# Seven-product gates: both partial sums as single-bank PSUM tiles, products in alternating order

## Chip, cores and metric

One core of a Trainium2 chip. The time is device microseconds (us) of one execution, and the median of several executions is compared. A profiled execution gives the trace; its span runs from its first to its last instruction.

## What is computed

A linear attention with random features (8 batches, 8 heads, 576 tokens, head size 64, 128 features) feeds a bilinear feed-forward layer over 4608 tokens:

```
phi(x) = exp(x @ omega.T - |x|^2/2 - max) / sqrt(m)
attn   = (phi(q) @ (phi(k).T @ v)) / (phi(q) @ sum(phi(k)) + 1e-6)
x      = attn as [4608, 512]
a, b   = x @ w1, x @ w2          # 512 -> 1024 each
out    = ((a * b) @ w3) @ w_out  # -> [4608, 512]
```

## The kernel before

The tokens are 36 chunks of 128. Each chunk goes through projection of q and k (tiles qpj and kpj), exponentials, the attention's quotient (tile nu), a split into fp16 high and low parts, a DMA transpose into xT, the gates (a and b, and their product) and the output projection (tile o, 24 matmuls of 128x512). The two last weights are multiplied into one matrix W at the start, while weights are converted; that head lasts until some 285 us.

Numbers are kept exact enough by splitting each operand in two fp16 parts and adding three products (PASSES). From chunk 8 on, two chunks at a time and one half i of the 1024 columns at a time (a "half pair", 28 in all), the gates use seven block products instead of eight: `seven_gate`. Each product is 24 matmuls of 128x128. Numbered in the order of the code before:

1. X = plain w1 blocks times X0; ACT copies X to s1 (snap, L1301)
2. W = plain blocks times X1; DVE adds W to s1 (plus, L1307)
3. X += sums 2 times B0; ACT copies X to u2 (L1301)
4. Y = sums 1 times A0
5. X += sums 3 times A1; ACT copies X to u3 (L1301), then DVE adds Y to u3 (L1305)
6. X += plain w2 blocks times B1; DVE multiplies s1 by X (L1340), and s1 is split into h
7. Y += sums 4 times C0; DVE adds Y to u2 (L1307), multiplies u2 by u3 (L1344, DVE or POOL), and u2 is split into h

Products 1, 2 and 6 read the weights from w12b; 3, 4, 5 and 7 read sums that lie in the arena. X and Y are the two banks of one PSUM tile xy with tag "pa" (shape 128 x 2 x 512 f32); W is a one-bank tile w with tag "pm". There are two pa buffers (four banks) and four pm buffers (four banks). Attention (qpj, kpj, nu, the k-v sums) takes pa buffers; output projections, norms, the first chunks' gates and filler matmuls ("warm", which keep PE running in the head where nothing is ready) take pm buffers.

The order of all instructions is written out ahead by a list scheduler (class Plan): each operation has costs per engine, what it reads and writes, the buffers it takes and a rank. At each instant an idle engine takes the ready operation of lowest rank whose buffers are free. Ranks are a base per chunk plus a shift per step from the table SHIFT. The scheduler keeps X and Y apart, as keys (xy, 0) and (xy, 1). Each engine then executes its list strictly in that order and waits on semaphores, which the tile framework sets from the tiles that an instruction reads and writes. Reads of gate results have the gate's rank less 1000, ahead of all else that is ready on their engine.

The small buffers u (two of them, for u2 and u3) and asb (two, for s1) are the other ones that gates hold.

Of the kernel before, what the change touches and what calls it, by code (L numbers as in the profile page):

```python
# [53 lines left out]
class Plan:  # L54
# [215 lines left out]
    "attend": [-140.6108, -1279.0332, 96.048, -814.6063, 46.0223, 565.0647, 888.1831, -189.2611, -1755.0403, -492.3028, -593.491, -657.8477, -700.7601, -33.1091, -308.4841, -242.0773, -417.6381, -346.2611, 1.1496, -638.2965, -706.1053, -102.5187, 7.911, 97.4165, -119.6369, -950.2856, -491.3768, 237.9438, 549.924, -177.7823, 68.1437, -180.35, 127.2563, 10.4704, -299.7041, -19.7196],  # L270
    "fetch": [-422.5336, -193.7664, -115.3316, -55.3051, -40.5138, -42.8211, -11.7789, -8.9557, 0.0, -10.1416, 3.4931, 0.0, -5.8054, -27.3038, -12.3339, -12.1842, 7.0423, 8.1052, 12.6868, -5.6312, 0.0, 1.5375, 21.7423],
    "gate": [84.4841, -9.8224, 184.0693, 825.4235, 328.6051, -313.6299, 281.3475, 611.0941, -290.9896, -117.7816, -64.9002, -270.3623, 1.1389, -19.5741, 3.9425, 16.0617, -2.4194, 4.5289, 0.0, 0.0, -13.2021, -13.3977, 0.0, 0.0, -30.4327, -0.4898, 0.0, 0.0, -27.3399, 22.7329, 0.0, 0.0, 3.0654, 10.6963, 0.0, 0.0, -96.6277, 1.1412, 0.0, 0.0, 6.7892, 20.0692, 0.0, 0.0, -108.4898, 7.294, 0.0, 0.0, 8.1194, 460.834, 0.0, 0.0, -155.6188, -94.2281, 0.0, 0.0, -181.6658, 83.4966, 0.0, 0.0, 99.2112, 1108.5741, 0.0, 0.0, 371.8924, 602.2299, 0.0, 0.0, -618.141, 814.4092],
# [9 lines left out]
    "out": [908.8765, 99.9845, 133.0496, -21.1332, -0.2109, 18.3999, 0.0586, 4.1794, -128.2247, -4.2684, -1.2544, -1.3084, -129.2248, 28.5423, 3.7214, 23.152, -1.7608, 11.9693, 12.9972, 547.9276, 861.8305, 278.0591, 393.7249, 61.9603, 499.264, 809.9431, 201.8663, -36.053, 36.4142, -127.9741, 1115.7242, 51.6774, 1069.562, 459.4601, 67.1902, 204.5781],  # L282
# [5 lines left out]
    "sum": [311.8865, -32.354, 244.6241, 473.4846],  # L288
    "unit": [-821.4058, -181.9305, -184.3904, -88.8633, -132.9001, -47.9472, -28.52, -5.7077, -171.7387, 20.0538, 28.6707, -182.3521, -50.1462, -60.8755, -11.3478, -7.7281, 80.6276, 111.3257, 279.8563, 284.0477, -32.0859, 306.7812, 422.9414, -290.3398, -63.7105],
    "v": [0.0, 0.0, 852.8931, -29.537, 21.5041, -411.0284, 56.0495, -1895.7559],  # L290
# [42 lines left out]
def tile_favor_attention_then_bilinear_ffn(  # L333
# [128 lines left out]
    def one(e, us, fn, **kw):  # L462
        return op([(e, us, fn)], **kw)
# [743 lines left out]
    sums = {}  # L1207
# [52 lines left out]
    def seven_gate(c0, i, rank):  # L1260

        xy, w = Buf("pa", f"xy_{c0}_{i}"), Buf("pm", f"w_{c0}_{i}")

        def plain(n, c):
            return lambda: w12[n][i][c], ("b", i, n * NC + c)
# [11 lines left out]
        def product(dst, key, ws, x, start, new=()):  # L1277
            xv, xkey = x

            def go():  # L1280
                for f in range(4):
                    mm = [(c, a, b) for c in range(2) for a, b in PASSES]
                    for j, (c, a, b) in enumerate(mm):
                        nc.tensor.matmul(  # L1284
                            dst()[:, f * P : (f + 1) * P], ws[c][0]()[:, a, f * P : (f + 1) * P], xv(c, b),
                            start=start and f == 0 and j == 0, stop=j == len(mm) - 1, skip_group_check=True,
                        )

            one(PE, 1.35, go, r=[x_[1] for x_ in ws] + [xkey] + (everything if xy in new else []), w=[key], new=new, rank=rank)

        X, Y, Wd = (lambda: xy.ap[:, 0]), (lambda: xy.ap[:, 1]), (lambda: w.ap)
        kx, ky, kw = (xy, 0), (xy, 1), (w, 0)
# [4 lines left out]
        def f32(b):  # L1297
            return b.ap

        def snap(t, scale):  # L1300
            one(ACT, 0.58, lambda: nc.scalar.mul(f32(t), X(), scale), r=[kx], w=[t], new=[t], rank=first)  # L1301
# [27 lines left out]
        product(X, kx, [plain(0, 0), plain(0, 1)], block("X", 0), True, [xy])  # L1329
# [349 lines left out]
```

## Time and profile before

| | us |
|---|---|
| median of 3 runs | 808.61 (807.83 to 812.87) |
| profiled execution, its time | 807.72 |
| its span | 805.7 |
| PE busy | 765.6 (95%) |
| DVE busy | 640.9 (80%) |
| ACT busy | 487.9 (61%) |
| POOL busy | 293.5 (36%) |

PE is TensorE's matmuls, DVE is VectorE, ACT is ScalarE, POOL is GpSimd. The rest of the profiled execution's time, 2.0 us, lies around the span. The mean granted TensorE clock is 0.994 of full speed.

### The profile page before, as it was taken

The numbers are of one execution on the slowest core, as the hardware profiler recorded it, in microseconds if no ns is written. First come the engines' busy times: TensorE is split into PE (matmuls) and PEld (weight loads), VectorE is DVE, ScalarE is ACT, GpSimd is POOL, SyncE is SP. The second block draws the span as 40 slices with busy tenths as digits, with TensorE's granted clock in tenths as the row PEclk, the third lists the DMA queues.
The fourth block names the chain that finished last, engine by engine and source line by source line (L and its number), as shares of the span: only waits on it lengthen the run. The fifth ranks groups of instructions, "written<-read, shape, count | busy, mean of one in ns | idle before, by whom it ended". The sixth has DMA issues, their size and how long they took to land.

```text
span 805.7 us, 24557 instructions
## 1 busy us (share of the span) xinstructions
PE 765.6 (95%) x10475; PEld 595.6 (74%) x10475; DVE 640.9 (80%) x1169; ACT 487.9 (61%) x948; POOL 293.5 (36%) x327
## 2 busy tenths in 40 slices
PE   9999999989999998999998999998999999999998
PEld 7845478866887677777967877785878877768874
DVE  6899998999968897898798897987688767576321
ACT  5675876687789878565865666654566534442222
POOL 2010146356435343354153433474344323132210
PEclk9899999999999999999999999999999999999999
DMA  9978863524545675356543555463425543433201
GB/s 332 293 224 273 231 170 42 120 55 112 126 88 145 132 153 106 68 100 126 134 93 86 108 114 112 93 113 78 89 55 117 89 76 72 67 92 61 47 15 53
DMA packets 166909, 93.82 MB, mean 116 GB/s; under 512 B 136976, under 2 KB 145296, under 8 KB 166800
## 3 DMA queue, kind: packets, MB, share of 16 engines
q1 hardware_dynamic: 158784, 79.60, 44.1%
q10 hardware_dynamic: 8016, 12.65, 4.9%
q8 instruction: 82, 1.34, 0.7%
q14 instruction: 27, 0.22, 0.1%
HBM read 49.50 MB, written 9.44 MB: 73 GB/s over the span
## 4 chain that ended last, share of the span: by engine, by line
PE 53%; DVE 22%; ACT 11%; DMA 7%; issue 5%; POOL 2%; POOLq 0%; SPq 0%; ACTq 0%; DVEq 0%
PE xy L1284 20%; PE o L1511 12%; PE wp L1131 4%; PE ab L1177 3%; PE w L1284 2%; PE kvp L804 2%; ACT junk L486 2%; DMA qraw<-qT 2%; DMA vraw<-v 2%; PE qpj L618 1%; PE nu L889 1%; PE kvp L751 1%; PE kpj L611 1%; DVE vhl L734 1%; ACT e_q L648 1%
## 5 line engine op out<-in xcount | busy, mean ns | idle before, releaser
L1284 PE MATMUL xy<-xT,arena 128*128 128x128 f16 x2688 | 166.2, 219 | 11.3 <-ACT asb_s L1301 9.8
L1284 PEld LDWEIGHTS <-arena 128*128 128x128 f16 x2688 | 154.0, 98 | 16.8 <-issue 13.6
L1284 PEld LDWEIGHTS <-w12b 128*128 128x128 f16 x2016 | 115.5, 98 | 18.4 <-issue 9.2
L1177 PE MATMUL ab<-xT,w12b 128*128 128x128 f16 (+1 forms) x1152 | 89.8, 240 | 3.1 <-ACT asb L1189 2.8
L1284 PE MATMUL xy<-xT,w12b 128*128 128x128 f16 x1344 | 84.3, 219 | 8.8 <-DVE u_u L1305 4.6
L1177 PEld LDWEIGHTS <-w12b 128*128 128x128 f16 x1152 | 82.2, 99 | 10.3 <-issue 4.2
L1511 PE MATMUL o<-Wb,w12b 128*128 128x512 f16 x384 | 88.3, 379 | 0.5 <-ACT o L1520 0.4
L1511 PEld LDWEIGHTS <-w12b 128*128 128x128 f16 x384 | 36.0, 98 | 40.8 <-issue 0.8
L1511 PE MATMUL o<-Wb 128*128 128x512 f16 x252 | 58.1, 379 | 0.0
L1511 PE MATMUL o<-Wb,arena 128*128 128x512 f16 x228 | 52.5, 379 | 2.1 <-DVE asb L1191 1.8
L1301 ACT ACTIVATE u_u<-xy 128x512 f32<-128x512 f32 x56 | 33.1, 590 | 35.4 <-PE xy L1284 33.9
L1340 DVE TENSOR_TENSOR asb_s<-xy,asb_s 128x512 f32<-128x512 f32 x28 | 19.3, 690 | 41.2 <-PE xy L1284 37.5
L669 POOL TENSOR_TENSOR ek<-e_k,ek 128x1024 f16<-128x1024 f32 x18 | 40.4, 2243 | 28.5 <-ACT ek L526 20.1
L631 DVE TENSOR_REDUCE nm_q<-qpj 128x8 f32<-128x1024 f32 x36 | 43.7, 1215 | 2.7 <-PE qpj L618 2.0
L631 DVE TENSOR_REDUCE nm_k<-kpj 128x8 f32<-128x1024 f32 x36 | 43.7, 1214 | 2.7 <-PE kpj L611 1.8
L669 POOL TENSOR_TENSOR eq<-e_q,eq 128x1024 f16<-128x1024 f32 x15 | 32.9, 2194 | 34.3 <-ACT eq L526 15.8
L1511 PEld LDWEIGHTS <-Wb 128*128 128x128 f16 x252 | 23.6, 98 | 27.2 <-issue 1.1
L1284 PE MATMUL w<-xT,w12b 128*128 128x128 f16 x672 | 42.1, 219 | 1.4 <-DVE asb_s L1307 1.4
L659 ACT ACTIVATE e_q<-e_q,ln_e,es_q 128x1024 f32<-128x1024 f32 x25 | 30.9, 1238 | 17.2 <-DVE e_q L655 13.9
L1520 ACT ACTIVATE o<-o,oscs 128x512 f32<-128x512 f32 x36 | 24.6, 682 | 27.3 <-PE o L1511 23.8
L1511 PEld LDWEIGHTS <-arena 128*128 128x128 f16 x228 | 21.3, 98 | 26.4 <-issue 2.7
L1305 DVE TENSOR_TENSOR u_u<-xy,u_u 128x512 f32<-128x512 f32 x28 | 19.2, 686 | 24.4 <-ACT u_u L1301 24.3
(235 smaller groups left out, 1644.2 us busy)
## 6 DMA issues: line engine op xcount, KB each, us to landing
vraw<-v SPq DMA_DIRECT2D x36, 260.0 KB, 3.5
qraw<-qT SPq DMA_DIRECT2D x36, 256.0 KB, 2.9
kraw<-kT SPq DMA_DIRECT2D x36, 256.0 KB, 3.2
out<-o SPq DMA_DIRECT2D x36, 256.0 KB, 2.2
arena<-w3T ACTq DMA_DIRECT2D x6, 1024.0 KB, 5.6
arena<-w ACTq DMA_DIRECT2D x6, 1024.0 KB, 5.4
arena<-wo SPq DMA_DIRECT2D x4, 1024.0 KB, 8.1
arena<-w3T SPq DMA_DIRECT2D x2, 1024.0 KB, 7.5
```

Source lines behind the costliest of these rows:

```text
L486: nc.scalar.activation(d, src, AF.Square, scale=pre, accum_out=dst)
L631: one(DVE, 1.22, lambda: nc.vector.tensor_reduce(nm.ap, pj(), AX.X, ALU.max, negate=True), r=[pa], w=[nm], new=[nm])
L659: one(ACT, 1.23, lambda: nc.scalar.activation(e.ap, e.ap, AF.Exp, scale=factor(), bias=ln_e), r=key, w=[e])
L669: engine(g).tensor_tensor(f16(t.ap)[:, 1], e.ap, f16(t.ap)[:, 0], ALU.subtract)
L1131: nc.tensor.matmul(bank.ap, w[:, j], guest[:, j], start=j == 0, stop=j == NF - 1)
L1177: nc.tensor.matmul(dst, w12[m][i][cc][:, a, r * P : (r + 1) * P], x.ap[:, b, cc, off : off + T], start=j == 0, stop=j == len(mm) - 1,)
L1284: nc.tensor.matmul(dst()[:, f * P : (f + 1) * P], ws[c][0]()[:, a, f * P : (f + 1) * P], xv(c, b), start=start and f == 0 and j == 0, stop ...
L1301: one(ACT, 0.58, lambda: nc.scalar.mul(f32(t), X(), scale), r=[kx], w=[t], new=[t], rank=first)
L1305: one(DVE, 0.69, lambda: nc.vector.tensor_tensor(f32(t), dst(), f32(t), ALU.add), r=[key], w=[t], rank=first)
L1340: one(DVE, 0.69, lambda: nc.vector.tensor_tensor(s1.ap, X(), s1.ap, ALU.mult), r=[kx], w=[s1], rank=first)
L1511: nc.tensor.matmul(bank.ap, hs[c, f][1]()[:, a], W[f][:, b], start=f0 + i == 0, stop=f0 + 4 == NF and i == len(mm) - 1,)
L1520: one(ACT, 0.67, lambda: nc.scalar.mul(o.ap, bank.ap, sc), r=[bank, ("osc", c)], w=[o], new=[o], rank=rank - 1000)
```

## The change

X and Y become two one-bank tiles of tag "pm", x and y, both taken by product 1. W goes away: product 2 writes Y, and product 4 starts Y again. The copy into u3 now reads Y after product 4, and the addition to u3 reads X after product 5 (before, the copy read X and the addition Y). Products 6 and 7 change places: the product with C0 into Y comes sixth and the one with B1 into X last. So the bank alternates X, Y, X, Y, X, Y, X. Numbers of matmuls, copies and additions stay, as do all buffer counts. Gates no longer take pa buffers. All entries of the table SHIFT have new values (left out but for two lines).

```diff
 SHIFT = {
-    "kv parts": [7.7168, 235.9384],
+    "kv parts": [-438.9681, -616.9088],
...
-    "sum": [311.8865, -32.354, 244.6241, 473.4846],
+    "sum": [482.7184, 151.9164, 140.7414, -351.1859],
...
     def seven_gate(c0, i, rank):
-        xy, w = Buf("pa", f"xy_{c0}_{i}"), Buf("pm", f"w_{c0}_{i}")
+        bx, by = Buf("pm", f"x_{c0}_{i}"), Buf("pm", f"y_{c0}_{i}")
...
-            one(PE, 1.35, go, r=[x_[1] for x_ in ws] + [xkey] + (everything if xy in new else []), w=[key], new=new, rank=rank)
-
-        X, Y, Wd = (lambda: xy.ap[:, 0]), (lambda: xy.ap[:, 1]), (lambda: w.ap)
-        kx, ky, kw = (xy, 0), (xy, 1), (w, 0)
+            one(PE, 1.35, go, r=[x_[1] for x_ in ws] + [xkey] + (everything if bx in new else []), w=[key], new=new, rank=rank)
+
+        X, Y = (lambda: bx.ap), (lambda: by.ap)
+        kx, ky = bx, by
...
-        def snap(t, scale):
-            one(ACT, 0.58, lambda: nc.scalar.mul(f32(t), X(), scale), r=[kx], w=[t], new=[t], rank=first)
+        def snap(t, scale, src=X, key=kx):
+            one(ACT, 0.58, lambda: nc.scalar.mul(f32(t), src(), scale), r=[key], w=[t], new=[t], rank=first)
...
-        product(X, kx, [plain(0, 0), plain(0, 1)], block("X", 0), True, [xy])
+        product(X, kx, [plain(0, 0), plain(0, 1)], block("X", 0), True, [bx, by])
         snap(s1, 2.0**-37)
-        product(Wd, kw, [plain(0, 2), plain(0, 3)], block("X", 1), True, [w])
-        plus(s1, Wd, kw, 2.0**-37)
+        product(Y, ky, [plain(0, 2), plain(0, 3)], block("X", 1), True)
+        plus(s1, Y, ky, 2.0**-37)
         product(X, kx, [(sums[2, i, c]) for c in range(2)], block("B", 0), False)
         snap(u2, 2.0**-37)
         product(Y, ky, [(sums[1, i, c]) for c in range(2)], block("A", 0), True)
+        snap(u3, 1.0, Y, ky)
         product(X, kx, [(sums[3, i, c]) for c in range(2)], block("A", 1), False)
-        snap(u3, 1.0)
-        plus(u3, Y, ky, 1.0)
+        plus(u3, X, kx, 1.0)
+        product(Y, ky, [(sums[4, i, c]) for c in range(2)], block("C", 0), False)
         product(X, kx, [plain(1, 2), plain(1, 3)], block("B", 1), False)
+        plus(u2, Y, ky, 2.0**-37)
         one(DVE, 0.69, lambda: nc.vector.tensor_tensor(s1.ap, X(), s1.ap, ALU.mult), r=[kx], w=[s1], rank=first)
         out_parts(c0, s1)
-        product(Y, ky, [(sums[4, i, c]) for c in range(2)], block("C", 0), False)
-        plus(u2, Y, ky, 2.0**-37)
```

## Rows read from the trace of the kernel before

**Rows 1.** The page, busy time, share of the span, instructions of PE.

```profile
PE   765.6 (95%) x10475; PEld 595.6 (74%) x10475; DVE 640.9 (80%) x1169; ACT 487.9 (61%) x948; POOL 293.5 (36%) x327
```

**Rows 2.** Table by stretch: length, busy time of each engine, granted clock, DMA.

```profile
0.00:285.00 285.00, 275.89 (x2909) 205.18 (x2910) 253.74 (x463) 209.91 (x477) 105.17 (x125) 0.98 0.62 167
285.00:805.70 520.70, 489.72 (x7570) 390.46 (x7566) 387.15 (x708) 277.95 (x471) 188.34 (x203) 1.00 0.43 89
...
800.00:805.70 5.70, 1.83 (x9) 0.63 (x7) 0.00 (x0) 0.70 (x2) 0.00 (x0) 0.99 0.24 92
```

**Rows 3.** Groups by line, PE: the filler matmuls (busy, mean ns, idle before).

```profile
L458 PE MATMUL warm<-ones 128*128 128x256 bf16 x127 | 18.0, 293 | 1.1 <-DVE unscaled L377 1.1
```

**Rows 4.** Who waited for whom, PE: us in total, times, longest.

```profile
PE xy L1284 <- ACT asb_s L1301: 9.8, 14, 0.7
PE xy L1284 <- DVE u_u L1305: 4.6, 6, 1.4
...
PE xy L1284 <- DVE e_q L655: 2.1, 1, 2.1
...
PE qpj L618 <- DVE xw_x L910: 1.6, 3, 0.9
PE w L1284 <- DVE asb_s L1307: 1.4, 1, 1.4
PE xy L1284 <- ACT u_u L1301: 1.1, 2, 0.7
...
PE xy L1284 <- ACT e_k L648: 0.7, 1, 0.7
PE xy L1284 <- DVE mx L923: 0.6, 1, 0.6
...
PE xy L1284 <- DVE xw_x L910: 0.5, 1, 0.5
```

**Rows 5.** Timeline near 698 us: start, length, engine, line; idle before and its releaser.

```profile
695.48 1.50 PE L1284 MATMUL xy<-xT,w12b 128*128 128x128 f16 x24
...
696.82 1.50 PE L1284 MATMUL xy<-xT,arena 128*128 128x128 f16 x24
...
698.16 1.50 PE L1284 MATMUL xy<-xT,w12b 128*128 128x128 f16 x24
698.36 0.69 DVE L1340 TENSOR_TENSOR asb_s<-xy,asb_s 128x512 f32<-128x512 f32 x1 [0.52 <-PE xy L1284]
...
699.50 1.50 PE L1284 MATMUL xy<-xT,arena 128*128 128x128 f16 x24
...
701.04 0.60 ACT L1301 ACTIVATE asb_s<-xy 128x512 f32<-128x512 f32 x1 [1.33 <-PE xy L1284]
...
701.69 1.50 PE L1284 MATMUL xy<-xT,arena 128*128 128x128 f16 x24 [0.69 <-ACT asb_s L1301]
```

**Rows 6.** Timeline near 712 us: a product behind a DVE read of the other bank.

```profile
711.37 0.60 ACT L1301 ACTIVATE u_u<-xy 128x512 f32<-128x512 f32 x1 [1.19 <-PE xy L1284]
...
712.52 0.68 DVE L1305 TENSOR_TENSOR u_u<-xy,u_u 128x512 f32<-128x512 f32 x1
...
713.26 1.50 PE L1284 MATMUL xy<-xT,w12b 128*128 128x128 f16 x24 [0.59 <-DVE mx L923]
```

**Rows 7.** Timeline near 728 us: reads of tile w and of tile xy.

```profile
726.27 1.50 PE L1284 MATMUL w<-xT,w12b 128*128 128x128 f16 x24
727.61 2.84 PE L1284 MATMUL xy<-xT,arena 128*128 128x128 f16 x48
727.88 0.69 DVE L1307 SCALAR_TENSOR_TENSOR asb_s<-w,asb_s 128x512 f32<-128x512 f32 x1 [0.47 <-PE w L1284]
...
730.49 0.60 ACT L1301 ACTIVATE u_u<-xy 128x512 f32<-128x512 f32 x1 [5.50 <-PE xy L1284]
731.14 1.50 PE L1284 MATMUL xy<-xT,arena 128*128 128x128 f16 x24 [0.69 <-ACT u_u L1301]
```

**Rows 8.** The page, groups by line: the multiplication that reads X (L1340).

```profile
L1340 DVE TENSOR_TENSOR asb_s<-xy,asb_s 128x512 f32<-128x512 f32 x28 | 19.3, 690 | 41.2 <-PE xy L1284 37.5
```

More of the change, by code (lines that the diff above doesn't have):

```diff
@@ L269 @@
 SHIFT = {
-    "attend": [-140.6108, -1279.0332, 96.048, -814.6063, 46.0223, 565.0647, 888.1831, -189.2611, -1755.0403, -492.3028, -593.491, -657.8477, -700.7601, -33.1091, -308.4841, -242.0773, -417.6381, -346.2611, 1.1496, -638.2965, -706.1053, -102.5187, 7.911, 97.4165, -119.6369, -950.2856, -491.3768, 237.9438, 549.924, -177.7823, 68.1437, -180.35, 127.2563, 10.4704, -299.7041, -19.7196],
-    "fetch": [-422.5336, -193.7664, -115.3316, -55.3051, -40.5138, -42.8211, -11.7789, -8.9557, 0.0, -10.1416, 3.4931, 0.0, -5.8054, -27.3038, -12.3339, -12.1842, 7.0423, 8.1052, 12.6868, -5.6312, 0.0, 1.5375, 21.7423],
@@ L272 @@
-    "gate": [84.4841, -9.8224, 184.0693, 825.4235, 328.6051, -313.6299, 281.3475, 611.0941, -290.9896, -117.7816, -64.9002, -270.3623, 1.1389, -19.5741, 3.9425, 16.0617, -2.4194, 4.5289, 0.0, 0.0, -13.2021, -13.3977, 0.0, 0.0, -30.4327, -0.4898, 0.0, 0.0, -27.3399, 22.7329, 0.0, 0.0, 3.0654, 10.6963, 0.0, 0.0, -96.6277, 1.1412, 0.0, 0.0, 6.7892, 20.0692, 0.0, 0.0, -108.4898, 7.294, 0.0, 0.0, 8.1194, 460.834, 0.0, 0.0, -155.6188, -94.2281, 0.0, 0.0, -181.6658, 83.4966, 0.0, 0.0, 99.2112, 1108.5741, 0.0, 0.0, 371.8924, 602.2299, 0.0, 0.0, -618.141, 814.4092],
[9 rows of a table removed]
@@ L282 @@
-    "out": [908.8765, 99.9845, 133.0496, -21.1332, -0.2109, 18.3999, 0.0586, 4.1794, -128.2247, -4.2684, -1.2544, -1.3084, -129.2248, 28.5423, 3.7214, 23.152, -1.7608, 11.9693, 12.9972, 547.9276, 861.8305, 278.0591, 393.7249, 61.9603, 499.264, 809.9431, 201.8663, -36.053, 36.4142, -127.9741, 1115.7242, 51.6774, 1069.562, 459.4601, 67.1902, 204.5781],
[5 rows of a table removed]
-    "sum": [311.8865, -32.354, 244.6241, 473.4846],
-    "unit": [-821.4058, -181.9305, -184.3904, -88.8633, -132.9001, -47.9472, -28.52, -5.7077, -171.7387, 20.0538, 28.6707, -182.3521, -50.1462, -60.8755, -11.3478, -7.7281, 80.6276, 111.3257, 279.8563, 284.0477, -32.0859, 306.7812, 422.9414, -290.3398, -63.7105],
@@ L290 @@
-    "v": [0.0, 0.0, 852.8931, -29.537, 21.5041, -411.0284, 56.0495, -1895.7559],
+    "attend": [-344.5336, -863.3505, -70.6144, -131.482, -1506.3662, -333.3574, -103.4191, 7.1947, 60.9253, -32.7535, 18.6681, -108.953, -558.1044, -52.2323, 382.9496, -190.0001, -104.0751, -91.4797, -646.8141, -687.6983, -37.7378, 211.8501, 1393.0138, 106.7495, -170.1491, -110.946, 57.5431, 184.7415, 56.0684, -192.3624, -91.951, -176.7992, 216.8146, 38.3368, -2248.693, -15.202],
+    "fetch": [-395.1367, -263.3025, -107.3478, -142.792, -36.362, -959.709, -14.3577, -14.5706, 0.0, -4.7734, 4.0789, 0.0, -17.9307, -10.2591, -11.7003, -3.8869, 17.9688, 18.5746, 3.5, 16.9483, 0.0, 12.1216, 13.06],
@@ new lines @@
+    "gate": [34.7804, -29.6444, -10.065, -89.002, -27.3084, -6.0439, 129.6502, -17.0297, 388.6957, -8.5912, 692.3104, 937.1265, 284.3371, -322.219, 193.869, 370.3877, 275.6107, 459.2977, 0.0, 0.0, 55.2125, 133.4596, 0.0, 0.0, 223.4237, 807.8211, 0.0, 0.0, -406.232, 4.2812, 0.0, 0.0, 16.9321, 150.1117, 0.0, 0.0, 56.867, 317.3446, 0.0, 0.0, 100.7986, 261.576, 0.0, 0.0, -46.2142, 104.0213, 0.0, 0.0, -222.6991, 208.6584, 0.0, 0.0, -991.9536, -55.2257, 0.0, 0.0, -325.8881, 255.4881, 0.0, 0.0, -16.8875, 305.8452, 0.0, 0.0, -15.2719, -18.917, 0.0, 0.0, -679.3126, 312.5891],
[9 rows of a table added]
@@ new lines @@
+    "out": [-20.132, -230.7836, -62.9796, 830.6893, 254.1977, 930.6871, 237.9168, -335.4428, 951.938, -341.3368, 808.7732, 348.4642, -130.897, 1115.6368, 71.106, -104.36, 322.1385, 263.4889, 289.4962, 10.9208, -596.5897, 394.1804, 557.7642, 49.388, -25.2456, 258.9955, 85.3124, -252.7556, 554.9951, 330.1611, -242.5933, 625.2243, -610.7126, -232.717, 496.3645, 207.0009],
[5 rows of a table added]
+    "sum": [482.7184, 151.9164, 140.7414, -351.1859],
+    "unit": [-747.9261, -719.9066, -200.9629, -717.993, -48.1889, -174.9094, -18.9419, -8.5076, -71.4105, -1.8121, 13.5129, -73.3507, -54.5629, -37.5469, -5.9012, 4.1535, 29.5488, 34.147, 20.2489, 96.7241, -353.4154, 184.6303, 287.0949, -149.1731, 4.9956],
@@ L291 @@
+    "v": [0.0, 0.0, 256.8978, 193.3537, 250.3211, -6.0913, -183.8097, -199.8197],
 }
```

26 rows, old and new, of the table SHIFT are left out of this document.

## The prediction, made before the change was run

> **What bounds the kernel now.** I first read the busy shares [rows 1]: PE works 765.6 us, 95% of the span of 805.7, DVE 80% and ACT 61%. So PE is the bound, and a gain must come out of its 40.1 us of idle time or out of work on it that serves nothing. The table by stretch [rows 2] splits that. Until 285 us, the head without seven-product gates, PE idles 285.0 - 275.9 = 9.1 us, and a further 18.0 us of its busy time are filler matmuls [rows 3]. From 285 us on it idles 520.7 - 489.7 = 31.0 us, of which 5.7 - 1.8 = 3.9 us are the very end, where the last outputs leave. The 27.1 us between are what a change to these gates can touch. DVE is at 253.7 of 285.0 in the head (89%) and 387.2 of 520.7 after it (74%).
>
> Next I read who waited for whom on PE [rows 4]. The gates' own tile xy leads: 9.8 us in 14 waits for ACT's copy into s1, 4.6 us in 6 for DVE's addition to u3, 1.1 us in 2 for ACT's copies into u2 or u3, and 0.6 us once behind a DVE line that has nothing to do with it.
>
> Then the timeline, to see why. At 695.48 begins product 6 (weights from w12b, into X), at 696.82 product 7 (arena, into Y) [rows 5]. Products follow each other every 1.34 us and each is drawn 1.50 long, so product 6 ends at 696.98. The multiplication that reads only X, hence only product 6, begins at 698.36, when product 7 has ended at 698.32. In the same rows product 1 of the next half pair runs from 698.16 and product 4 from 699.50; ACT's copy of X, due at 699.66, begins at 701.04, as product 4 ends (701.00). Product 3 needs that copy, so PE stands idle for 0.69 us. A read of X thus waits for whatever was last issued into the tile, though that went to the other bank. It holds the other way too [rows 6]: product 6 (713.26) needs the copy that ended at 711.97, yet it begins 0.06 us after DVE's addition, which reads Y and ends at 713.20.
>
> Tile w is the control [rows 7]. Product 2 into w begins at 726.27 and ends at 727.77. DVE's read of w begins at 727.88 with two xy products (3 and 4) running from 727.61; the copy of X, whose product was the first of those two, begins at 730.49, after both. So the wait belongs to the shared tile, not to PE's order. The Trainium skill, "PSUM — Partial Sum Buffer", section "PSUM bank collisions raise a hardware error", tells us to guard by bank, and X and Y were two banks already. By that rule alone the split would have nothing to remove and the sum would be 0; the rows differ, since the waits are there, set by the tile.
>
> **Part 1: separate tiles.** Removed: the waits of PE for a copy or addition that was itself held back by the other bank, or that concerned only the other bank: 9.8 + 4.6 + 1.1 + 0.6 = 16.1 us [rows 4]. All of this is PE idle time on the bound, and nothing else covers it. DVE and ACT are freed as well: the multiplication's queue stood 37.5 us behind xy products in 28 instances [rows 8]. I book nothing for that; it is the cover for part 3. Bounds: 0 if none of it goes, and no more than the whole 27.1 us.
>
> **Part 2: gates leave the pa buffers.** Before, xy keeps one of two pa buffers for most of a half pair, and projections, quotients and gates wait for one another's. The waits of this kind are xy for DVE's reads of projections and quotients or ACT's exponentials (2.1 + 0.7 + 0.5 us) and qpj for the quotient (1.6 us) [rows 4], together 4.9 us. I take all of it as gone for the gates' and projections' sake; a few could be plain lateness of DVE, so the bounds are 0 and 4.9.
>
> **Part 3: the alternating order.** Matmuls, copies and additions are as many as before, so busy time stays. Every bank now rests for one product before it is written again. The cover is 1.34 us less the 0.16 by which a product's drawn end overlaps the next, 1.18 us. ACT's copy takes 0.60 and hands over in 0.05 (701.64 to 701.69), DVE's addition 0.69 and the same [rows 5]: margins of 0.53 and 0.44 us if the engine is free at that moment. Before, product 6 had to wait for the copy of what product 5 had just written; that bare 0.69 is gone. Added is a wait: product 4 now needs DVE's addition of product 2 (before, W had its own tile), and product 7 still needs DVE's addition to u3, so 2 x 28 = 56 hand-overs by DVE have a margin of 0.44 us. Behind a waiting product stands all that is queued on PE, output projections too. The trace of before doesn't show these waits. The nearest row is the addition to u3, 6 waits of 28, 4.6 / 6 = 0.77 us each [rows 4]. Bounds: 0, and all 56 at 0.77, 43.1 us; below nothing they can't go, since a wait gives no time back. I take six such waits again, 4.6 us: the 6 of before were partly the false kind, and DVE has lost its own false holds.
>
> The copy into u3 comes one product earlier and holds its u buffer 1.34 us longer. The chain that frees the other one (product with C0, addition, multiplication, split) also begins one product earlier, so I cost it at nothing; if not covered, it is one product per half pair. At the very end the first chunk's h comes a product later and the second's earlier; its price is at most 1.34 us, and output projections lie between.
>
> **Part 4: new ranks.** They reorder everything, the head too: loads, conversions, DMA transposes, and where PE finds nothing ready. In the head no gate of this kind runs; what they could win is its 9.1 + 18.0 = 27.1 us of idle and filler, what they could lose has no row. I take 0, and half of that slack, 13.5 us, either way as a bound, since DVE at 89% sets that stretch and its work is the same.
>
> **Sum.** -16.1 - 4.9 + 4.6 + 0 = -16.4 us. Span 805.7 to 789.3; with 2.0 us around it 791.3. The profiled execution (807.7) is 0.9 us below the median of the runs (808.6), so a median of 792.
>
> **Rivals.** *DVE's hand-overs become the bound* (the slower side). Place: products 4 and 7, each 0.44 us of margin behind an engine that is busy three quarters of the time with instructions of 0.69 us and longer. From the 21.0 us that parts 1 and 2 give, 27 of 56 waits at 0.77 us eat all of it, and 38 make the kernel slower by 1%; all 56 give 808.6 - 21.0 + 43.1 = 831. For it: the second such hand-over is new. Against it: 22 of 28 had no wait even with a shared tile, and other PE work lies between most products.
>
> *The pm buffers run short.* Product 1 now takes two of the four at once, while an output projection holds one and the half pair before holds two; then it waits for that one's last DVE read. The price is the 0.69 us of a read and 0.05 us of hand-over per half pair where nothing fills it [rows 5], 28 x 0.74 = 20.7 us, so 792 + 21 = 813. For it: the gates went from three banks that they share with attention's buffers to a pool that the outputs use. The one wait of a product into w, 1.4 us, was already one for its bank to be read [rows 4]. Against it: pm carried little but w, norms and outputs in this stretch, and projections and quotients no longer compete and can fill. The Trainium skill, "Perfetto Trace Analysis", section "Matmul Optimizations", wants all eight banks in use; here the busiest stage is confined to four of them. By that rule this rival would be likelier than I make it; the trace before has no stretch in which gates live on four banks.
>
> *The new ranks spoil the head* by half its slack: 792 + 13.5 = 806. For it: the head's order is set by DVE and all ranks moved. Against it: no operation of the head changes.
>
> *The change doesn't do what it says*: reads still wait for the product issued last. Then part 1 and the cover of part 3 fall away: 808. The control with w [rows 7] speaks against it.
>
> **How the numbers follow.** Measurements of this kernel tell about 1% (8 us) from no change. The forecast (780 to 800) has 0.62, the hand-overs 0.12 (above 816), the short pm buffers 0.12 (800 to 813), the spoiled head 0.09 and no effect 0.05 (both within 1%). So faster 0.62, same 0.26, slower 0.12. The range: its low end is parts 1 and 2 without new waits, 808.6 - 21.0 = 787.6, less half of the filler, 9.0, so 779; its high end is the pm rival, 813. Outside lie the hand-overs and some 0.05 of a still better plan.
>
> **What will show it.** In the trace after, L1340's successor should begin when its own product ends, with the other bank's product running, and the 14 waits of 0.7 us for the copy into s1 should be gone; PE's idle time from the first such gate to the end should be near 15 us, not 31. Waits of products for DVE's additions (L1305, L1307) show part 3; above 27 of them the forecast falls. Waits of a half pair's first product for a DVE multiplication or an output's copy show short pm buffers. Filler and idle time before the first gate show part 4. The prediction is wrong if PE's idle time moves to other lines by as much as it left these.

## The result, and the profile after

The changed kernel takes 778.48 us (median of 4 runs, 777.76 to 780.06) against 810.06 us for the kernel before on the same chip: ratio 0.961, 95% interval 0.957 to 0.965. That is 3.9% faster, nearly twice the gain that the forecast of 792 meant, and half a microsecond below the range. The profiled execution's span is 776.8 us, 28.9 us less than before.

The page of the changed kernel, busy times (answers to [rows 1]):

```profile
PE 751.6 (97%) x10456; PEld 589.3 (76%) x10456; DVE 642.6 (83%) x1189; ACT 490.1 (63%) x951; POOL 262.8 (34%) x304
```

The table by stretch of the changed kernel, cut where its first seven-product gate begins (columns as in [rows 2]):

```profile
0.00:287.70 287.70, 271.87 (x2921) 199.13 (x2922) 259.36 (x467) 214.32 (x485) 85.97 (x120) 1.00 0.60 164
287.70:776.80 489.10, 479.76 (x7538) 390.17 (x7536) 383.25 (x723) 275.80 (x468) 176.84 (x185) 1.00 0.46 95
```

The same cut of the kernel before lies at 282.63 us (its first product 1 begins there):

```profile
0.00:282.63 282.63, 273.52 (x2866) 202.81 (x2867) 251.50 (x455) 207.60 (x473) 102.88 (x124) 0.98 0.61 167
282.63:805.70 523.07, 492.09 (x7613) 392.83 (x7609) 389.38 (x715) 280.26 (x476) 190.62 (x204) 1.00 0.44 89
```

The gates' stretch fell from 523.1 to 489.1 us. PE's idle time in it fell from 31.0 to 9.3 us, of which some 4 us are the end; the prediction had looked for about 15. But PE's busy time also fell, by 12.3 us, though the program has the same matmuls but for 19 fillers fewer, all of them in the head. About 5.4 us of that moved into the head, which now holds one output projection (24 matmuls, 5.2 us) and 120 k-v matmuls (3.6 us) more, and two products 2 (2.7 us) and one quotient (0.7 us) less. Otherwise the head has 6.7 us more of PE's idle time (9.1 to 15.8), 3.1 us less filler, and some 4 us less busy time on the rest (an estimate: 273.5 + 5.4 - 3.1 against 271.9), which goes with a granted clock of 0.98 on average before and 1.00 after. These three about cancel: the head is 5.1 us longer, nearly what moved into it, and on balance the 28.9 us came out of the gates' stretch. The other 7 us of busy time are the subject of a point below.

Who waited for whom on PE, changed kernel, over the whole span (answers to [rows 4]):

```profile
PE nu L889 <- DMA eqT<-eq: 4.0, 4, 1.3
...
PE x L1284 <- ACT u_u L1301: 1.1, 2, 0.7
...
PE x L1284 <- DVE u_u L1305: 0.9, 2, 0.7
...
PE y L1284 <- DVE asb_s L1307: 0.6, 1, 0.6
```

The 14 waits for the copy into s1 are gone, and so are the waits of gates for projections and quotients. Of the 56 hand-overs by DVE that the prediction feared, three show a wait, 1.5 us in all. What now leads, the quotient's wait for a DMA transpose, has nothing to do with the gates.

The timeline of the changed kernel in one half pair (answers to [rows 5]; product 3 in the numbering of before is the first line):

```profile
696.76 1.50 PE L1284 MATMUL x<-xT,arena 128*128 128x128 f16 x24
...
698.11 1.50 PE L1284 MATMUL y<-xT,arena 128*128 128x128 f16 x24
...
698.43 0.57 ACT L1301 ACTIVATE u_u<-x 128x512 f32<-128x512 f32 x1
...
699.45 1.50 PE L1284 MATMUL x<-xT,arena 128*128 128x128 f16 x24
699.64 0.60 ACT L1301 ACTIVATE u_u<-y 128x512 f32<-128x512 f32 x1 [0.35 <-PE y L1284]
...
700.78 1.50 PE L1284 MATMUL y<-xT,arena 128*128 128x128 f16 x24
701.06 0.69 DVE L1305 TENSOR_TENSOR u_u<-x,u_u 128x512 f32<-128x512 f32 x1 [0.42 <-PE x L1284]
...
702.12 1.50 PE L1284 MATMUL x<-xT,w12b 128*128 128x128 f16 x24
702.33 0.69 DVE L1307 SCALAR_TENSOR_TENSOR u_u<-y,u_u 128x512 f32<-128x512 f32 x1 [0.58 <-PE y L1284]
```

The reader should see five products at 1.34 us each with no gap, and each read beginning some 0.03 to 0.2 us after its own product's drawn end while the other bank's product runs: the copy of x at 698.43 for the product that ends at 698.26, the copy of y at 699.64 for the one that ends at 699.61.

### The profile page after: what moved, and what is told of

It reads as the page before. It is cut to its first block, busy times and chain, and to the rows that moved or that the text cites. A ratio compares the mean times of both kernels' runs of the same rounds, so it can differ in the third digit from the quotient of the medians.

```text
span 776.8 us, 24553 instructions
## 1 busy us (share of the span) xinstructions
PE 751.6 (97%) x10456; PEld 589.3 (76%) x10456; DVE 642.6 (83%) x1189; ACT 490.1 (63%) x951; POOL 262.8 (34%) x304
## 3 DMA queue, kind: packets, MB, share of 16 engines
q8 instruction: 82, 1.34, 0.7%
## 4 chain that ended last, share of the span: by engine, by line
PE 44%; DVE 34%; DMA 9%; ACT 6%; issue 5%; SPq 0%; POOL 0%; ACTq 0%; DVEq 0%
PE o L1511 14%; PE x L1284 12%; PE y L1284 9%; PE ab L1177 3%; DVE nm_q L631 3%; DVE arena L1051 2%; DMA eqT<-eq 2%; DVE eq L669 2%; DVE nm_k L631 2%; PE nu L889 2%; PE qpj L618 2%; DMA arena<-wo 1%; DVE w12b L1060 1%; DMA kraw<-kT 1%; PE kvp L804 1%
## 5 line engine op out<-in xcount | busy, mean ns | idle before, releaser
L1284 PEld LDWEIGHTS <-w12b 128*128 128x128 f16 x2016 | 114.6, 98 | 5.2 <-issue 1.2
L1177 PEld LDWEIGHTS <-w12b 128*128 128x128 f16 x1152 | 80.3, 98 | 9.8 <-issue 3.9
L1284 PE MATMUL x<-xT,arena 128*128 128x128 f16 x1344 | 84.2, 219 | 1.1 <-ACT u_u L1301 1.1
L1284 PE MATMUL y<-xT,arena 128*128 128x128 f16 x1344 | 84.2, 219 | 0.6 <-DVE asb_s L1307 0.6
L1284 PE MATMUL x<-xT,w12b 128*128 128x128 f16 x1344 | 83.5, 219 | 0.9 <-DVE u_u L1305 0.9
L1511 PEld LDWEIGHTS <-w12b 128*128 128x128 f16 x384 | 36.2, 98 | 41.9 <-issue 2.2
L631 DVE TENSOR_REDUCE nm_k<-kpj 128x8 f32<-128x1024 f32 x36 | 43.8, 1217 | 10.1 <-PE kpj L618 5.1
L669 POOL TENSOR_TENSOR ek<-e_k,ek 128x1024 f16<-128x1024 f32 x17 | 37.2, 2187 | 15.8 <-ACT ek L526 13.5
L1284 PE MATMUL y<-xT,w12b 128*128 128x128 f16 x672 | 42.1, 219 | 0.0
L1305 DVE TENSOR_TENSOR u_u<-x,u_u 128x512 f32<-128x512 f32 x28 | 19.2, 686 | 27.1 <-PE x L1284 26.2
L889 PEld LDWEIGHTS <-eqT 128*128 128x128 f16 (+1 forms) x936 | 29.7, 100 | 10.1 <-DMA eqT<-eq 5.3
L889 PE MATMUL nu<-kv,eqT 128*128 128x65 f16 (+1 forms) x936 | 32.7, 194 | 4.8 <-DMA eqT<-eq 4.0
```

Source lines behind the costliest of these rows:

```text
L631: one(DVE, 1.22, lambda: nc.vector.tensor_reduce(nm.ap, pj(), AX.X, ALU.max, negate=True), r=[pa], w=[nm], new=[nm])
L669: engine(g).tensor_tensor(f16(t.ap)[:, 1], e.ap, f16(t.ap)[:, 0], ALU.subtract)
L889: nc.tensor.matmul(n_[r0:r1, h // 4, h % 4], f16(t.ap)[:, x, place(h), r0:r1], kv_view(kvs[b])[:, y, h], start=n == 0, stop=n == 2,)
L1177: nc.tensor.matmul(dst, w12[m][i][cc][:, a, r * P : (r + 1) * P], x.ap[:, b, cc, off : off + T], start=j == 0, stop=j == len(mm) - 1,)
L1284: nc.tensor.matmul(dst()[:, f * P : (f + 1) * P], ws[c][0]()[:, a, f * P : (f + 1) * P], xv(c, b), start=start and f == 0 and j == 0, stop ...
L1305: one(DVE, 0.69, lambda: nc.vector.tensor_tensor(f32(t), dst(), f32(t), ALU.add), r=[key], w=[t], rank=first)
```

## Experiments

Three theories were to be told apart. Theory 1: the waits set by the shared tile cost the time. Theory 2: the new list of instructions (ranks, freed pa buffers) made the gain. Theory 3: the alternating order did. No run has the new gates, with their two pm tiles, at the old ranks.

**e1: the kernel before, the waits between the two banks not set.** Every engine's list is that of the kernel before: the two traces hold the same lines and tiles in the same order. Each read of a bank is declared independent of the products into the other, and each product of the reads of the other.

```diff
+        made = [([], []), ([], [])]; untie = lambda key, m, wr=False, a=0, z=0: key[0] is xy and ([tc.declare_no_dep(m.ins, o.ins, reason="other bank") for o in made[1 - key[1]][wr]], made[key[1]][not wr].append(m))
...
-                        nc.tensor.matmul(
+                        untie(key, nc.tensor.matmul(
...
-            one(ACT, 0.58, lambda: nc.scalar.mul(f32(t), X(), scale), r=[kx], w=[t], new=[t], rank=first)
+            one(ACT, 0.58, lambda: untie(kx, nc.scalar.mul(f32(t), X(), scale)), r=[kx], w=[t], new=[t], rank=first)
```

> The kernel before, with the same list of instructions on every engine; only the waits between one bank of tile xy and the other are not set. Theory 1 (the shared tile cost most of the 29 us): the 24 waits that the prediction counts go, 16.1 us, and each restart of PE gives back the 0.16 us by which it would have overlapped, 3.8 us more: about 789 us, 2.4% under the kernel before. Theory 2 (the new list of instructions, that is the ranks and the freed pa buffers, made the gain): at most 5 us, 804 us or more. Theory 3 (the alternating order made it): like theory 2, as the order of products stays.

Measured: 782.14 us, ratio 0.969 (0.963 to 0.976), 26.8 us less, and 7 us below what theory 1 had expected. Theories 2 and 3 fall as the main cause: neither order, ranks nor buffers changed. The timeline of e1 at the moment of [rows 5]:

```profile
671.75 1.51 PE L1284 MATMUL xy<-xT,w12b 128*128 128x128 f16 x24
...
673.10 1.50 PE L1284 MATMUL xy<-xT,arena 128*128 128x128 f16 x24
...
674.03 0.68 DVE L1340 TENSOR_TENSOR asb_s<-xy,asb_s 128x512 f32<-128x512 f32 x1
674.44 1.50 PE L1284 MATMUL xy<-xT,w12b 128*128 128x128 f16 x24
...
675.78 2.84 PE L1284 MATMUL xy<-xT,arena 128*128 128x128 f16 x48
...
675.98 0.60 ACT L1301 ACTIVATE asb_s<-xy 128x512 f32<-128x512 f32 x1 [0.61 <-PE xy L1284]
```

The multiplication no longer waits for product 7 (673.10 to 674.60), and the copy of X begins 0.04 us after its product's end (675.94), with products 4 and 3 following each other as 48 matmuls without a gap. The tables by stretch and of waits on PE of e1:

```profile
0.00:279.40 279.40, 268.43 (x2861) 198.88 (x2866) 251.40 (x455) 207.66 (x473) 103.85 (x124) 0.99 0.62 169
279.40:776.30 496.90, 486.35 (x7613) 391.90 (x7609) 388.43 (x715) 279.71 (x476) 187.32 (x204) 1.00 0.47 94
```

```profile
PE w L1284 <- DVE asb_s L1307: 1.4, 1, 1.4
PE xy L1284 <- DVE e_q L655: 1.3, 1, 1.3
...
PE xy L1284 <- ACT e_k L648: 0.6, 1, 0.6
PE xy L1284 <- ACT u_u L1301: 0.3, 1, 0.3
```

With the same 7613 matmuls, the gates' stretch went from 523.07 to 496.90 us, 26.2 us less: 20.4 us of idle time (31.0 to 10.55) and 5.7 us of busy time (492.09 to 486.35).

**e2: the changed kernel, with the waits of a shared tile put back.** Same list as the changed kernel; a read of x or y also waits for the last product issued into the other tile, and a product for the last read of the other. The cut shows the helper and one of the places where it is put around an instruction.

```diff
+        made, dep = {}, lambda m, o: o and tc.add_manual_dep(m.ins, o.ins.name, mybir.DependencyInfo(mybir.DependencyClass.Sync, mybir.DependencyReason.DATA)); tie = lambda key, m, wr=False, a=1, z=1: (a and [dep(m, made.get((k, not wr))) for k in (bx, by) if k is not key], z and made.update({(key, wr): m}))
...
-                        nc.tensor.matmul(
+                        tie(key, nc.tensor.matmul(
```

> The changed kernel, same list of instructions, with waits added as if x and y were one tile: a read of one also waits for the last product issued into the other, a product into one for the last read of the other. Theory 1: worse than before, since in the alternating order every read is followed by a product into the other bank; with half of the 6 hand-overs of a half pair bare, 28 x 3 x 0.85 us = 71 us, about 850 us; at least 800. Theory 2 or 3 (list or order hold the gain by themselves): below 790 us.

Measured: 863.12 us, ratio 1.068 (1.065 to 1.072), where theory 1 had expected about 850: the waits alone turn the faster kernel into one 6.8% slower than before. Its waits on PE:

```profile
PE x L1284 <- DVE u_u L1305: 15.3, 18, 0.9
PE y L1284 <- ACT u_u L1301: 15.1, 22, 0.7
PE x L1284 <- ACT u_u L1301: 10.1, 15, 0.7
PE y L1284 <- DVE asb_s L1307: 7.2, 8, 1.3
PE x L1284 <- ACT asb_s L1301: 7.0, 10, 0.7
```

Under the tie, then, the alternating order holds no gain; it suffers more from a shared tile than the old one, 84.6 us against the 26.8 of e1. That each read is here followed at once by a product into the other bank would explain it.

**e3 and e4: the changed kernel's order and ranks in one pa tile, tied and untied.** The list is made anew for both, because gates take a pa buffer again; it is the same list in e3 and e4. The cut shows what both have in common; e4 has the untying of e1 besides.

```diff
-        bx, by = Buf("pm", f"x_{c0}_{i}"), Buf("pm", f"y_{c0}_{i}")
+        xy = Buf("pa", f"xy_{c0}_{i}")
...
-        X, Y = (lambda: bx.ap), (lambda: by.ap)
-        kx, ky = bx, by
+        X, Y = (lambda: xy.ap[:, 0]), (lambda: xy.ap[:, 1])
+        kx, ky = (xy, 0), (xy, 1)
```

> The changed kernel's order of products and its ranks, but X and Y are the two banks of one pa tile again (so the list of instructions is made anew). Theory 1: the waits of the shared tile come back, 820 us or more. Theory 2 with ranks as the cause: below 795 us. Theory 3: the alternating order keeps its gain, below 795 us.

> As the one before, same list of instructions, with the waits between the two banks not set. Theory 1: near the changed kernel, 778 to 790 us, the rest being the pa buffers that gates and attention share again (the prediction had 4.9 us for them). Theory 2 with the freed pa buffers as the cause: 795 us or more.

Measured: e3 905.18 us (ratio 1.120, 1.116 to 1.124), e4 815.63 us (1.011, 1.007 to 1.014). The tie again costs some 90 us in this order. The number that theory 1 gave for e4, 778 to 790, was missed by 26 us; taken alone, 815.63 is in the range of theory 2 with the freed pa buffers as the cause (795 or more). The waits of e4 on PE (gates for DVE's reads of projections and quotients, and projections in turn) are of the kind in which gates and attention share buffers:

```profile
PE xy L1284 <- DVE e_q L655: 3.8, 2, 2.5
PE xy L1284 <- DVE xw_x L910: 3.6, 2, 2.3
PE kpj L618 <- DVE e_q L655: 3.1, 2, 2.7
PE xy L1284 <- ACT asb_s L1301: 2.9, 3, 2.1
```

Whether this is the price of shared pa buffers or of ranks that were made for another shape, e4 can't tell, as both differ from the changed kernel. Two other runs speak against the buffers as the cause of the gain: in e1 the gates still take pa buffers and the time is 782.14, and the gates of e4 with the old ranks (e8 below) are 17 us faster than with the new ones.

**e5: the kernel before with the new ranks alone.** The table SHIFT is the changed kernel's, all else that of before.

> The kernel before with the changed kernel's table of ranks alone: old gates, shared tile xy, old order of products; the list of instructions is made anew. Theory 1 (shared tile): the waits stay, and the ranks were made for other buffers, so 805 us or more. Theory 2 (ranks): below 795 us.

Measured: 865.72 us, ratio 1.067 (1.061 to 1.073). Theory 2 with the ranks alone as the cause falls: on the old gates the new ranks cost 56 us.

**e6 and e7: the two directions of the tie apart.** Same list as before. In e6 only reads are freed from the other bank's products, in e7 only products from the other bank's reads; the edit is that of e1 with one condition more, shown cut short for e6; e7 has `wr == True` there.

```diff
-[... for o in made[1 - key[1]][wr]]
+[... for o in made[1 - key[1]][wr] if wr == False]
```

> The kernel before, same list; only reads of one bank no longer wait for products into the other, products still wait for reads of the other bank. The prediction's rows put 9.8 + 1.1 us of PE's waits on reads held back (and 37.5 us of a DVE queue), 4.6 + 0.6 us on products held back by a read of the other bank. If the two are separate: 9.8 + 1.1 us and 16 restarts of 0.16 us, 13.5 us less, about 795 us. If the products' waits were long only because the reads came late, nearly all of the 27 us: about 784 us.

> The counterpart: same list, only products no longer wait for reads of the other bank; reads still wait for products of the other. If the two are separate: 4.6 + 0.6 us and 7 restarts, 6.3 us less, about 802 us. If the reads' waits are the cause of both: within 4 us of the kernel before.

Measured: e6 788.85 us (0.975, 0.972 to 0.979), e7 805.59 us (0.996, 0.994 to 0.998). 20.4 us lie with reads held back by the other bank's products, 3.6 us with products held back by the other bank's reads; the forecasts for separate causes were 13.5 and 6.3. Neither reading fits alone: e7 lies just within the 4 us that were expected if the reads' waits cause both, and e6 lies between the two numbers expected, 795 if separate and 784 if not. In e7 the leading wait stays as in [rows 4]; in e6 three of the six waits for the addition to u3 are left, so a part of the products' waits came of late reads:

```profile
PE xy L1284 <- ACT asb_s L1301: 10.1, 15, 0.7
```

```profile
PE xy L1284 <- DVE u_u L1305: 2.8, 3, 1.5
```

**e8: the new order in one pa tile, old ranks, untied.** The gates of e4 with the old table.

> The changed kernel's order of products in one pa tile, with the ranks of before, and the waits between the two banks not set; the list is made anew. If the alternating order is worth something by itself: below the untied kernel before, under 778 us. If order is worth nothing once the waits are gone: 780 to 800 us, by how well old ranks fit. If a list made anew with ranks that were not made for it costs more than order can give: 800 us or more, as the new ranks in one pa tile (816 us).

Measured: 798.82 us, ratio 0.987 (0.983 to 0.991), in the range expected if order is worth nothing. So no sign that the alternating order is worth something by itself once the waits are gone; it lies 17 us above e1, which has the old order with the same ranks, and how much of that is the list made anew is open.

**e9 and e10: the changed kernel as it is and the kernel of e1, side by side on one chip.**

> The changed kernel as it is, on the same chip and beside the same runs of the kernel before as the next one, to see whether order, freed pa buffers and new ranks give anything beyond the removed waits. If the removed waits are all: the two medians within 3 us of each other, 778 to 783 us. If the rest gives something of its own: 3 us or more under the untied kernel before.

> The untied kernel before once more: 779 to 785 us; compared with the changed kernel of the same call.

Measured: the changed kernel 781.31 us (0.964, 0.960 to 0.967), the untied kernel before 782.75 us (0.966, 0.963 to 0.968). The medians are 1.4 us apart, within the 3 us expected if the removed waits are all, and the intervals overlap. On the whole time, order, freed buffers and ranks together add nothing that can be told. By stretch the two kernels do differ. From the first seven-product gate on, e9 and then e10:

```profile
295.75:783.13 487.38, 479.81 (x7540) 390.13 (x7536) 382.03 (x722) 276.08 (x467) 176.35 (x185) 1.00 0.47 96
```

```profile
283.97:780.98 497.01, 486.40 (x7609) 391.92 (x7608) 388.57 (x714) 279.87 (x476) 187.32 (x204) 1.00 0.47 94
```

With the 5.4 us of work that the changed kernel does in its head, its gates' stretch is 492.8 against 497.0 us here, and 494.5 against 496.9 in the first pair of traces (the result and e1). So order, buffers or ranks gained some 2 to 4 us there, and the head, longer in the changed kernel even without those 5.4 us (290.4 against 284.0 here), took as much or more. Which of the three gained it is open, and so is how much of the longer head is clock.

## Why the prediction was wrong, point by point

*The bound and the mechanism* were right. PE's idle time in the gates' stretch was the place, the waits came from the shared tile, and the control with tile w [rows 7] had told so; e1 and e2 show it from both sides.

*Part 1 is the step that failed, by its size.* It booked 16.1 us, the idle time in front of the gates' products whose named releaser was a gate's read or a DVE line just behind one. The waits removed from the same list gave 26.2 us in the gates' stretch (e1). Two things were missed.

First, a wait costs more than the idle time that the row shows. In [rows 5] product 4 begins at 699.50 and product 3 at 701.69: 2.19 us where 1.34 would do, 0.85 lost, but the row says 0.69. The missing 0.16 us is the overlap of one product's drawn end (1.50) with the next start; I knew of it, since the copy's margin in part 3 is worked out with it, and left it out of part 1. Between the kernel before and e1, the idle times listed in the PE timeline of the gates' stretch fall from 36 with 25.8 us to 9 with 6.3 us, and 5.7 us of busy time go with those 27: 0.21 us each. In e2 97 stand in place of 10 of the changed kernel:

```profile
288.94:861.11 572.17, 493.98 (x7540) 393.35 (x7536) 381.16 (x721) 275.84 (x467) 176.61 (x184) 1.00 0.40 81
```

Against the changed kernel its gates' stretch is 83.1 us longer and PE's idle time in it 68.9, so 14.2 us or 0.16 each are of this kind.

Second, the tie's delay spread into waits that are listed under other lines. The named ones fell from 16.1 to 0.3 us in e1, but idle time fell by 20.4. The rest, 4.6 us, stood under other lines: the projections' waits for the quotient (1.6 to nothing), the quotient's for the addition to u2 (0.9 to nothing), gates for DVE's exponential input (2.1 to 1.3) and so on. I had called DVE's 37.5 us of queue time behind xy products [rows 8] mere cover and booked nothing; it is 37.5 us in 21 waits, not in 28, and 16.1 us in 11 are left of it in e1. That the spread went by this queue is argued, not tested apart; e6, which frees only the reads, gives 20.4 of the 26.8 us.

*Part 2* booked 4.9 us for freed pa buffers. In e1, where gates still share pa, only 1.9 us of those waits are left (1.3 + 0.6; 2.4 in e10, the same kernel); some 3.0 us were the tie's. Only what is left can be the buffers', and on the whole time e9 with e10 doesn't show even that.

*Part 3* booked 4.6 us of new waits for DVE; measured 0.9 + 0.6 = 1.5 us in 3 of 56. The margin of 0.44 us held, with DVE at 383 of 489 us in that stretch. That its reads go ahead of all else ready and that it lost its false holds would explain it; no run tests this.

*Part 4* booked nothing for the ranks. Its sign was filler and idle time before the first gate. They were 18.0 + 9.1 = 27.1 us before and are 14.9 + 15.8 = 30.7 after, 3.6 us worse, well within its bound of 13.5; a better clock in the head made up for it in this execution.

```profile
L458 PE MATMUL warm<-ones 128*128 128x256 bf16 x108 | 14.9, 293 | 2.3 <-DVE asb L1191 1.3 <-DVE unscaled L377 1.1
```

e5 adds that the new ranks are of no use to the old gates.

*The sum* was -16.4 against -28.9 us, 12.5 short. Part 1 fell short by 10.1, and part 3 booked 3.1 us of waits too many. But 3.0 of part 2's 4.9 us lie within the 26.2 of e1 and can't be counted again. With 26.2 us for the removed waits and 1.5 for the new ones, 4.2 of the 28.9 us are left, which no run assigns to buffers, order, ranks or clock.

*The rivals* did not come about: neither DVE's hand-overs nor short pm buffers (no first product waits for a read of the half pair before), nor a head spoiled by 13.5 us; and the reads do begin with the end of their own products. The Trainium skill, "PSUM — Partial Sum Buffer", section "PSUM bank collisions raise a hardware error", guards by bank, so that two banks may be used independently. e1 agrees: without the waits between banks the kernel before is 3.1% faster. The Trainium skill, "Perfetto Trace Analysis", section "Matmul Optimizations", wants all eight banks in use. Both kernels use all eight; gates that keep to the four pm banks and gates that take pa and pm banks do equally well on the whole time (e9, e10).

*The range* failed at its low end, which left the waits' spread and the overlap out.

## What to carry to other kernels

Give accumulators that are written and read at different times tiles of their own, even if they lie in different banks already: here one two-bank tile made each copy wait for a product that it never read, and without that wait the kernel takes 3.4% less (e10). To see it in a trace, look for a read that begins when the next product ends and not its own, and hold it against a tile that isn't shared. And price a wait on PE, whose products overlap, by the distance between starts, not by the idle time in front: 0.85 against 0.69 us here, plus what the held engine's queue passes on.

## What the runs showed of the hardware

The same program, profiled twice, had spans of 776.8 and 783.1 us (the changed kernel, and e9). The difference arose in the head, with PE's granted clock. In the first execution it was at full speed, 2.4 GHz, throughout the head. In e9 it was at half, the 1.2 GHz level, in two stretches. The first lies between 14 and 18 us (0.57 on average there): the same 30 filler matmuls took 3.45 us in the first execution and 5.12 us in e9.

```profile
13.93 3.45 PE L458 MATMUL warm<-ones 128*128 128x256 bf16 x30
```

```profile
14.14 5.12 PE L458 MATMUL warm<-ones 128*128 128x256 bf16 x30
```

The second lasts from 38 to 55 us. Tables by stretch from 40 to 50 us, the first execution and then e9:

```profile
40.00:50.00 10.00, 10.00 (x73) 7.29 (x73) 9.76 (x24) 5.04 (x14) 1.10 (x1) 1.00 0.78 262
```

```profile
40.00:50.00 10.00, 10.00 (x48) 9.64 (x46) 7.84 (x22) 5.55 (x14) 0.63 (x1) 0.50 0.34 108
```

Shortly before it, PE had stood idle for 1.95 us (waiting for ACT's exponentials) until 36.41 us. The same matmuls, and a norm behind them, in the first execution and then in e9:

```profile
34.23 1.16 PE L611 MATMUL kpj<-o_om_raw,kraw 64*128 64x128 f32 x16 [1.64 <-ACT ek_f L648]
...
39.55 0.16 PE L492 MATMUL norm_kv<-sums_kv,ones 128*128 128x1 bf16 x1
```

```profile
36.41 1.16 PE L611 MATMUL kpj<-o_om_raw,kraw 64*128 64x128 f32 x16 [1.95 <-ACT ek_f L648]
...
44.51 0.21 PE L492 MATMUL norm_kv<-sums_kv,ones 128*128 128x1 bf16 x1
```

So e9 was 2.2 us behind before the second stretch and 5.0 us at the norm. At the first seven-product gate it was 8.1 us behind (295.75 against 287.68), and 6.3 at the end. In the two places where e9 waited 1.64 us (before 13.04 us) and 1.95 us, the first execution had waits of 1.20 and 1.64 us and kept its clock. Why the one kept it and the other didn't is not shown.
